# Taking the gate's column out of a matrix product: row sums on VectorE, POOL and ScalarE instead, and another order of work in the first output chunks

## The chip, the cores and the metric

The kernel runs on one core of a Trainium2 chip. The metric is the device time of one execution in microseconds (us). The engines of a core run their own instruction queues side by side: TensorE (PE in the profile, with PEld for its weight loads), VectorE (DVE), ScalarE (ACT), GpSimd (POOL) and SyncE (SP, which issues most of the transfers here). They wait for one another through semaphores.

## The reference

```python
def _A_ref(x, wqkv, wo):              # B, S, D = 1, 2048, 448; 16 heads of 28
    q, k, v = split_heads(x @ wqkv)
    pq, pk = phi(q), phi(k)           # phi(t) = where(t > 0, t + 1, exp(t)) + 1e-6
    kv = einsum("bhsd,bhse->bhde", pk, v)
    z = sum over s of pk
    o = (pq @ kv) / (pq . z + 1e-6)
    return merge_heads(o) @ wo

def _B_ref(u, ...):                   # S4D: a long causal convolution per column, plus u * D_skip
    ...

x = A_x
g = sigmoid((x * gate_w).sum(-1, keepdims=True))
return g * _A_ref(x, ...) + (1 - g) * _B_ref(x, ...)
```

There are 2048 rows of x with 448 columns. The gate g is one number for each row: a weighted sum of the row, put through a sigmoid. The change concerns how that weighted sum is computed.

## The kernel before

**Tiling.** The 2048 rows are handled as 16 chunks of 128 rows. Each chunk of x is loaded twice over in one transfer: turned (columns on the partitions, for use as a matmul operand) and plain (rows on the partitions). A float32 operand is split in a high part (a cast to the reduced format float32r, on ScalarE) and a low part (the rest, by a subtraction, mostly on POOL), and a product is made of three kinds of matmuls: high by high, low by high, high by low. One product of a chunk by a 448 x 448 matrix is 11 matmuls of 448 columns.

**The first stage** is a loop over c = 2 to 13, with the chunks before and after written out by hand. In iteration c the queues get, in this order:
- SP: the load of x for chunk c + 3 (`load_x`).
- PE: the k product of chunk c + 1 (11 matmuls), the q product of chunk c (11 matmuls), then `do_g` of chunk c (11 matmuls, which accumulate k's features times x in four PSUM banks).
- ACT and POOL: high and low parts of chunk c + 2 (`split_t` for the turned copy, `split_n` for the plain one), POOL's product of x with D_skip (`skip`).
- ACT and DVE: k's features of chunk c + 1 (`k_feature`, `k_high`, `k_low`) and q's of chunk c (`q_post`).
- DVE, in iterations 2 to 5: the preparation of the S4D part (`steps`), which ends with four small transposes on PE (line 319); in iterations 6 to 11 a running sum over chunks (`running`).

The order within each engine's queue is the order of the source (`manual_schedule`); a queue does not go on past an instruction that waits.

**Buffers.** x lies in a pool of four buffers (`xp`). Chunks 0, 1 and 2 share two of them: the first holds the turned chunk 2 and the plain chunk 0, the second the plain chunks 1 and 2. Chunks 3 and 4 have the other two, and the load of chunk 5 in iteration 2 needs one of these four again. A buffer is given out again when the last instruction that reads it, on whichever engine, is done. The k product goes to one of two PSUM banks (`v1` or `k`: in iterations 3, 5, 6 and 7 it is `k`), and the q product to one bank (`q`); the next product in the bank waits until the features are finished with it.

**The gate** is column 448 of the q product: the weights of q have 450 columns, with `gate_w` as column 448 and zeros in 449. `q_post` starts with ACT's exponential of that column into `e1[:, c]` (line 387); `gate(0, 15)` turns 15 columns of `e1` into 1 + exp(-s) and the factor `og` after the first stage, and the last chunk's follow in `late`, in the middle of the output stage.

**Between the stages**, `norm_a` to `norm_d` make the denominators and the normalised q of each chunk (POOL products, DVE reductions and reciprocals), and kv is multiplied by `wo` (`kv_products`, `m_products`). The 11 matmuls of the last q product are cut in pieces (`q_run`) and put where PE would otherwise wait.

**The output stage** goes over pairs of chunks (c, c + 1). Each pair is turned on PE (`turn_pe`), split in high and low parts (ACT and DVE: `turn_even`, `odd_high`, `odd_ends`, `odd_low`), multiplied in `attend` (11 matmuls of 448 columns for each chunk, line 676), and combined with the S4D part and sent out by `final_b` (DVE, SP).

Of the kernel before, what the change touches and what calls it, by code (L numbers as in the profile page):

```python
# [15 lines left out]
P = 128  # L16
S = 2048
D = 448
# [12 lines left out]
FIRST = 2 * NAT + J * D  # L31
QA = 1
QW = 512
# [108 lines left out]
@with_exitstack  # L142
def gated_mix_kernel(ctx: ExitStack, tc: tile.TileContext, xin, wq_d, wvo_d, abc_d, ldt_d, dsk_d,
                     turn_d, cst_d, first_d, gin_d, out):
# [24 lines left out]
    ones = const.tile([P, P], F32R, name="ones")  # L169
    dsk = const.tile([P, D], F32, name="dsk")  # L170
    side = []
# [33 lines left out]
    raw = yf[:, F0:]  # L205
    wqr = yf[:, F0 - J * (D + 2):F0].rearrange("p (j d) -> p j d", j=J)
    abc = [t[:DJ, o:o + 2 * J * N].rearrange("p (i j n) -> p i j n", i=2, j=J) for t, o in ((pf, 3 * J * N), (rf, 0))]
# [44 lines left out]
    def skip(c):  # L252
        POOL.tensor_tensor(out=y[:, c], in0=plain[c][:, :D], in1=dsk, op=ALU.mult)  # L253

    idle = ps.tile([P, 512], F32, name="q", tag="q")
# [88 lines left out]
    def project(*args, **kw):  # L344
        o, run = pieces(*args, **kw)
        run(11)
        return o
# [38 lines left out]
    def q_post(c, o, mid=None):  # L386
        ACT.activation(e1[:, c:c + 1], o[:, D:D + 1], AF.Exp, scale=-1.0)
        if c < 5 or c >= NC - 2:
            return feature(pq[:, c], o, mid, side[0][:, :D] if 1 < c < 5 else None)
        e = tp.tile([P, D], F32, name="e", tag="e")  # L390
        ACT.activation(e, o[:, :D], AF.Relu, scale=-1.0)
        ACT.activation(e, e, AF.Exp, scale=-1.0)
        ACT.add(e, e, 1e-6)
        DVE.scalar_tensor_tensor(out=pq[:, c], in0=o[:, :D], scalar=C1, in1=e, op0=ALU.add, op1=ALU.max)

    def do_q(c, tag="q"):
        q_post(c, project(c, wqh, wql, D + 2, tag))

    def gate(a, b):
        DVE.tensor_scalar(out=e1[:, a:b], in0=e1[:, a:b], scalar1=1.0, scalar2=None, op0=ALU.add)  # L400
        DVE.reciprocal(out=og[:, a:b], in_=e1[:, a:b])
        DVE.tensor_scalar(out=og[:, a:b], in0=og[:, a:b], scalar1=-1.0, scalar2=1.0, op0=ALU.mult, op1=ALU.add)

# [94 lines left out]
    k_low(2)  # L498
    qo = project(0, wqh, wql, D + 2, "q", "w")
    split_t(3)  # L500
    q_post(0, qo)
    split_n(2)
    qo = project(1, wqh, wql, D + 2, "v0")
    q_post(1, qo)
# [13 lines left out]
    for c in range(2, NC - 2):  # L518
# [12 lines left out]
        ko = project(c + 1, wkh, wkl, D, "v1" if c in (2, 4) or c > 6 and c % 2 == 0 else "k")  # L531
        rows = list(ROWS.get(c, ()))
        if c > 6 and rows:
            running(rows.pop(0))
        if c == 13:
# [17 lines left out]
        k_low(c + 1)  # L553
        if rows:
            running(rows.pop(0))
        qo = project(c, wqh, wql, D + 2, "q")
        q_post(c, qo)
        for i in rows:
            running(i)
        if c < 5:  # L560
            steps(2 if c == 4 else 1)
# [73 lines left out]

    def turn_even(c, o):
        t = xt_p.tile([P, 2, J, P], F32R, name="th", tag="t")
        th[c], tl[c] = t[:, 0], t[:, 1]
        ov = o.rearrange("p (j t) -> p j t", j=J)
        ACT.copy(th[c], ov)  # L640
        DVE.tensor_tensor(out=tl[c], in0=ov, in1=th[c].bitcast(F32), op=ALU.subtract)  # L641

    def turn_odd(c, o, oe):
        odd_high(c, o)
        odd_ends(c, 0, oe)
        odd_ends(c, 1, oe)
        odd_low(c, o)

# [16 lines left out]
    def attend(c, cuts):  # L665
        av[c] = []
        even = c // 2 * 2
        h, l, ends = th[c], tl[c], (th, tl)[c % 2][even + 1][:, 3]
        for i, (lo, hi) in enumerate(cuts):
            pool, tag = ((p3, "a"), (p3, "a"), (ps, "v0"), (ps, "k"))[(c + i) % 4]  # L670
            a = pool.tile([P, 512], F32, name="a", tag=tag)
            av[c].append((a, lo, hi))
            seq = [(u_[:, j], w_[:, j]) for j in (2, 0, 1) for u_, w_ in ((h, mh), (l, mh), (h, ml))]
            seq += [(ends, mh[:, 3]), (tl[even][:, 3], low_w3[c % 2])]
            for n, (u_, w_) in enumerate(seq):
                PE.matmul(a[:, lo:hi], lhsT=u_, rhs=w_[:, lo:hi], start=n == 0, stop=n == 10)  # L676
# [22 lines left out]
    zl = tp.tile([P, D], F32R, name="zl", tag="v0", bufs=1)  # L699
    qo = project(c, wqh, wql, D + 2, "q")  # L700
    do_g(c, (0, 1, 2))
# [9 lines left out]
    norm_a(1)  # L711
    gate(0, c + 1)
    norm_bd(0)
    norm_c(0)
    norm_a(2)
    for i in range(4):
        do_g(c + 1, (i,))
        ACT.copy(gs[i], g[i][:, :D])
        if i == 1:
            qo, q_run = pieces(c + 1, wqh, wql, D + 2, "q")  # L720
            q_run(2)
# [54 lines left out]

    q_run(1)
    k1 = kv_products(1)
# [21 lines left out]
    norm_a(4)  # L800
    turn_even(0, t0)
    odd_high(1, t1)
# [19 lines left out]
    def late():  # L822
        c = NC - 1
        yield
        e = tp.tile([P, D], F32, name="e", tag="e")
        t = tp.tile([P, D], F32, name="t", tag="t")
        ACT.activation(e1[:, c:], qo[:, D:D + 1], AF.Exp, scale=-1.0)
        ACT.activation(e, qo[:, :D], AF.Exp)
        yield
        DVE.tensor_scalar(out=e1[:, c:], in0=e1[:, c:], scalar1=1.0, scalar2=None, op0=ALU.add)  # L830
        DVE.tensor_scalar(out=t, in0=e, scalar1=1.0, scalar2=1e-6, op0=ALU.min, op1=ALU.add)
        DVE.reciprocal(out=og[:, c:], in_=e1[:, c:])
        yield
        DVE.tensor_scalar(out=og[:, c:], in0=og[:, c:], scalar1=-1.0, scalar2=1.0, op0=ALU.mult, op1=ALU.add)
        DVE.scalar_tensor_tensor(out=pq[:, c], in0=qo[:, :D], scalar=C1, in1=t, op0=ALU.add, op1=ALU.max)
# [7 lines left out]
    norm_b(5)  # L843
    norm_d(4, 2, ACT.copy)
    for c in range(2, NC, 2):
        more = c + 2 < NC
        final_b(c - 2)
        t0 = turn_pe(c)
        t1 = turn_pe(c + 1)
        if more:  # L850
            norm_c(c + 2)
        if c + 6 < NC:
            norm_a(c + 6)
        if c + 4 < NC:
            norm_b(c + 4)
        turn_even(c, t0)
        if more:
            norm_c(c + 3)
        if c + 6 < NC:
            norm_a(c + 7)  # L860
        turn_odd(c + 1, t1, t0)
# [28 lines left out]
def _layout(inputs):  # L890
# [16 lines left out]
    def tiles(w):  # L907
# [7 lines left out]
    w = np.asarray(inputs["A_wqkv"])  # L915
    wq = np.zeros((D, D + 2), np.float32)
    wq[:, :D] = w[:, :D]
    wq[:, D] = np.asarray(inputs["gate_w"])
    byd = lambda a: np.asarray(a).reshape(J, DJ, -1).transpose(1, 0, 2)
# [21 lines left out]
        f(byd(inputs["B_log_dt"])[:, :, 0]),  # L941
        f(np.asarray(inputs["B_D_skip"]).reshape(1, D)),
        f(np.stack([np.eye(P), lag >= 1], axis=1)),
# [20 lines left out]
```

## Time and profile before

| | |
|---|---|
| median of 3 runs | 168.7 us (168.25 to 168.81) |
| the profiled execution: its own time | 168.38 us |
| its span in the trace | 166.4 us |
| PE busy | 161.1 us, 97% of the span |
| DVE, ACT, POOL busy | 116.1, 109.4, 104.9 us |
| mean granted clock of PE | 0.997 of full |

All times within the execution count from the start of the span. The execution's own time is 2.0 us longer than the span, for what lies around it. A line of a timeline gives the start in us, the duration in us, the engine, the source line, the operation, output <- inputs with their shapes, the count of merged instructions, and in brackets the idle time of the engine ahead of it with the instruction that ended it. A line of the chain gives start, length, engine, tensor and source line. Matmuls overlap in the pipeline: one takes about 0.36 us, and the next starts 0.20 us after it.

### The profile page before, as it was taken

How to read it: one execution, taken by the hardware profiler on the slowest of the kernel's cores; microseconds unless marked ns; L12 is line 12 of the kernel's file. 1: busy time of each engine (PE TensorE's matmuls, PEld its weight loads, DVE VectorE, ACT ScalarE, POOL GpSimd, SP SyncE). 2: the span in 40 equal slices, each digit the busy share in tenths (PEclk: the TensorE clock that was granted, in tenths of full speed). 3: DMA queues.
4: the chain of work that ended last, by engine and by line, in shares of the span. 5: the costliest groups of instructions: out<-in, count | busy, mean ns of one | idle time of the engine just before them, and what ended most of it. 6: DMA issues, size and time to landing. Idle time of an engine off the chain costs nothing.

```text
span 166.4 us, 2609 instructions
## 1 busy us (share of the span) xinstructions
PE 161.1 (97%) x835; PEld 144.9 (87%) x835; DVE 116.1 (70%) x243; ACT 109.4 (66%) x257; POOL 104.9 (63%) x116
## 2 busy tenths in 40 slices
PE   6999999999999999999999999999999999999991
PEld 2698999999999999999999999988987999999990
DVE  0837753685852879889885555898899979986441
ACT  3688668988486784766758966453856766676541
POOL 3073589678809449477295999749689998633000
PEclk9999999999999999999999999999999999999998
DMA  5999966687974330959988007997121221122222
GB/s 157 411 314 321 287 143 230 228 295 276 336 255 136 126 107 19 221 141 250 295 261 165 0 4 117 185 203 161 27 46 55 110 110 55 61 110 110 110 78 95
DMA packets 10783, 27.51 MB, mean 165 GB/s; under 512 B 1328, under 2 KB 6992, under 8 KB 10544
## 3 DMA queue, kind: packets, MB, share of 16 engines
q1 hardware_dynamic: 8992, 21.71, 39.1%
q0 software_dynamic: 1632, 5.51, 17.6%
q8 instruction: 7, 0.11, 0.3%
q10 hardware_dynamic: 144, 0.11, 0.2%
q14 instruction: 8, 0.07, 0.1%
HBM read 17.87 MB, written 3.67 MB: 129 GB/s over the span
## 4 chain that ended last, share of the span: by engine, by line
PE 87%; DVE 6%; DMA 2%; ACT 1%; issue 1%; ACTq 0%; DVEq 0%
PE g L416 21%; PE q L340 19%; PE a L676 19%; PE v L340 12%; PE k L340 11%; PE tr L633 3%; DMA y<-in 2%; DVE den L601 2%; PE k L755 1%; DVE wk L743 1%; DVE th L641 1%; DVE ot L681 1%; ACT kvh L772 0%; DVE shl L743 0%; ACT wk L466 0%
## 5 line engine op out<-in xcount | busy, mean ns | idle before, releaser
L676 PE MATMUL a<-wk,th 128*128 128x448 f32 (+1 forms) x178 | 37.4, 357 | 0.3 <-DVE th L641 0.3
L416 PE MATMUL g<-pkh,xn 128*128 128x448 f32 x112 | 35.7, 364 | 0.0
L676 PEld LDWEIGHTS a<-wk,th 128*128 128x128 f32 x178 | 31.3, 188 | 2.9 <-DVE th L641 0.7
L237 POOL TENSOR_TENSOR xt<-xr,xt 128x512 fp32r<-128x512 f32 x14 | 18.2, 1298 | 19.8 <-ACT xt L241 19.8
L340 PE MATMUL q<-wqh,xt 128*128 128x450 f32 x120 | 27.8, 367 | 0.0
L237 POOL TENSOR_TENSOR xn<-xr,xn 128x448 fp32r<-128x448 f32 x16 | 19.6, 1228 | 10.1 <-ACT xn L247 10.1
L340 PEld LDWEIGHTS q<-wqh,xt 128*128 128x128 f32 x120 | 22.5, 189 | 1.8
L416 PE MATMUL g<-pkl,xn 128*128 128x448 f32 x64 | 23.3, 364 | 0.0
L416 PEld LDWEIGHTS g<-pkh,xn 128*128 128x128 f32 x112 | 21.1, 188 | 2.3
L596 POOL TENSOR_TENSOR prod<-pq,zb 128x448 f32<-128x448 f32 x16 | 18.3, 1154 | 4.5 <-ACT zb L709 2.9
L253 POOL TENSOR_TENSOR y<-xr,dsk 128x448 f32<-128x448 f32 x16 | 20.4, 1281 | 0.0
L340 PE MATMUL k<-wk,xt 128*128 128x448 f32 x88 | 19.7, 366 | 0.1
L340 PE MATMUL v<-wk,xt 128*128 128x448 f32 x88 | 18.9, 362 | 0.0
L340 PEld LDWEIGHTS k<-wk,xt 128*128 128x128 f32 x88 | 16.4, 188 | 2.0 <-ACT wk L466 0.5
L340 PEld LDWEIGHTS v<-wk,xt 128*128 128x128 f32 x88 | 16.5, 188 | 1.1
L681 DVE SCALAR_TENSOR_TENSOR ot<-y,og,a 128x448 f32<-128x448 f32 (+1 forms) x17 | 10.7, 626 | 7.5 <-PE a L676 7.3
L621 POOL TENSOR_TENSOR room<-pq,den 128x336 f32<-128x336 f32 x16 | 12.1, 756 | 5.4 <-issue 2.6
L687 ACT COPY pq<-a 128x448 f32<-128x448 f32 (+1 forms) x17 | 8.6, 512 | 5.8 <-DVE ot L681 5.6
L416 PEld LDWEIGHTS g<-pkl,xn 128*128 128x128 f32 x64 | 11.2, 174 | 1.1 <-DVE pkl L379 0.2
L656 ACT CAST th<-tr 64x128 fp32r<-64x128 f32 x32 | 8.3, 261 | 5.5 <-DVE th L641 5.1
L340 PE MATMUL q<-wql,xt 128*128 128x450 f32 x45 | 11.7, 366 | 0.0
L369 DVE SCALAR_TENSOR_TENSOR k<-k,e 128x448 f32<-128x448 f32 x8 | 5.1, 632 | 9.0 <-ACT e L368 8.8
(155 smaller groups left out, 289.7 us busy)
## 6 DMA issues: line engine op xcount, KB each, us to landing
xr<-in SPq DMA_DIRECT2D x15, 512.0 KB, 3.9
out<-ot SPq DMA_DIRECT2D x15, 224.0 KB, 1.9
room<-in SPq DMA_DIRECT2D x3, 896.0 KB, 7.5
wvo<-in SPq DMA_DIRECT2D x2, 896.0 KB, 5.5
y<-wvo POOLq DMA_DIRECT2D x2, 896.0 KB, 8.2
y<-room POOLq DMA_DIRECT2D x2, 896.0 KB, 9.2
y<-over POOLq DMA_DIRECT2D x2, 896.0 KB, 9.5
y<-in SPq DMA_DIRECT2D x2, 480.0 KB, 4.7
```

Of the source, the lines that this page charges most:

```text
L237: eng.tensor_tensor(out=o, in0=r, in1=h.bitcast(F32), op=ALU.subtract)
L253: POOL.tensor_tensor(out=y[:, c], in0=plain[c][:, :D], in1=dsk, op=ALU.mult)
L340: PE.matmul(o[:, :n], lhsT=a, rhs=b, start=run.n == 1, stop=not seq)
L369: DVE.scalar_tensor_tensor(out=pks[c], in0=pks[c], scalar=1.0, in1=e, op0=ALU.add, op1=ALU.max)
L416: PE.matmul(g[i][:a.shape[1], :D], lhsT=a, rhs=b, start=c == 0 and n == 0, stop=c == NC - 1 and n == len(seq) - 1)
L596: POOL.tensor_tensor(out=pd[c], in0=pq[:, c], in1=zb, op=ALU.mult)
L621: POOL.tensor_tensor(out=n[:, :3, :DJ].rearrange("p j (h d) -> p j h d", h=4), in0=a, in1=r[:, :H - 4].rearrange("p (j h) -> p j h", j=3)[ ...
L633: PE.transpose(o[:, j * P:(j + 1) * P], pn[c][:, j], ident)
L656: ACT.copy((th, tl)[i][c][half, 3], oe[i * DT:(i + 1) * DT, 3 * P:])
L676: PE.matmul(a[:, lo:hi], lhsT=u_, rhs=w_[:, lo:hi], start=n == 0, stop=n == 10)
L681: DVE.scalar_tensor_tensor(out=ot[:, lo:hi], in0=y[:, c, lo:hi], scalar=og[:, c:c + 1], in1=a[:, lo:hi], op0=ALU.mult, op1=ALU.add)
L687: ACT.copy(pq[:, c, lo:hi], a[:, lo:hi])
```

## The change

The gate's column leaves the q product, whose matmuls then have 448 columns instead of 450, and `gate_w` is loaded as a second row beside D_skip and spread over the partitions (`rows`, `gwt`). The weighted sum of a row is computed from the plain x in one of two ways:
- `gate_sum(c)` on DVE: one instruction that multiplies and sums along the row. Chunks 0 and 1 in iteration 2, chunks 2 and 3 in iteration 3, chunks 4 and 5 in iteration 4, chunk 14 in iteration 12, chunk 15 in iteration 13, each behind `q_post` of that iteration.
- `gate_products(c + 2)` on POOL at the end of iterations 4 to 11, and `gate_total(c + 1)` on ACT at the head of iterations 5 to 12, ahead of `split_t`: chunks 6 to 13.

One exponential of all 16 columns and one `gate()` follow the first stage; the parts for the last chunk in `late` go. In the second place the order of work changes: in the first output pairs the high parts are made earlier and the low part of chunk 2 stands ahead of `final_b`; `norm_d(2, 2)` and `norm_d(4, 2)` move; the 11 matmuls of `attend(0)` get another order; one more of the last q product's matmuls goes ahead of `kv_products`. The padding of one buffer changes, so that the sizes together stay as they were.

```diff
-PADS = 32
+PADS = 96
+SUMS = {2: (0, 1), 3: (2, 3), 4: (4, 5), 12: (14,), 13: (15,)}
...
-    wqh, wql = (const.tile([P, J, QW], F32R, name=n)[:, :, :D + 2] for n in ("wqh", "wql"))
+    wqh, wql = (const.tile([P, J, D], F32R, name=n) for n in ("wqh", "wql"))
...
-    SP.dma_start(out=dsk, in_=dsk_d.to_broadcast([P, D]))
+    SP.dma_start(out=rows, in_=rows_d.to_broadcast([P, 2, D]))
     load_x(3)
...
+    def gate_sum(c):
+        DVE.scalar_tensor_tensor(out=tp.tile([P, D], F32, name="t", tag="t"), in0=plain[c][:, :D], scalar=1.0, in1=gwt,
+                                 op0=ALU.mult, op1=ALU.mult, accum_out=e1[:, c:c + 1])
+
+    def gate_products(c):
+        POOL.tensor_tensor(out=prod[:, c % 3], in0=plain[c][:, :D], in1=gwt, op=ALU.mult)
+
+    def gate_total(c):
+        ACT.activation(prod[:, c % 3], prod[:, c % 3], AF.Copy, accum_out=e1[:, c:c + 1])
...
     def q_post(c, o, mid=None):
-        ACT.activation(e1[:, c:c + 1], o[:, D:D + 1], AF.Exp, scale=-1.0)
...
         ko = project(c + 1, wkh, wkl, D, "v1" if c in (2, 4) or c > 6 and c % 2 == 0 else "k")
...
+        if 4 < c < 13:
+            gate_total(c + 1)
...
-        qo = project(c, wqh, wql, D + 2, "q")
+        qo = project(c, wqh, wql, D, "q")
         q_post(c, qo)
...
+        for i in SUMS.get(c, ()):
+            gate_sum(i)
         if c < 5:
             steps(2 if c == 4 else 1)
...
+        if 3 < c < 12:
+            gate_products(c + 2)
...
-    gate(0, c + 1)
+    ACT.activation(e1, e1, AF.Exp, scale=-1.0)
+    gate()
...
-    q_run(1)
+    q_run(2)
     k1 = kv_products(1)
...
-    turn_even(0, t0)
+    even_high(0, t0)
     odd_high(1, t1)
...
+    norm_d(2, 2, ACT.copy)
     ACT.copy(mh[:DT, 3], shl[:DT, 0].bitcast(F32))
+    even_low(0, t0)
     odd_ends(1, 0, t0)
-    norm_d(2, 2, ACT.copy)
...
+            if c == 0:
+                seq = [seq[n] for n in (0, 2, 3, 6, 1, 4, 5, 7, 8)]
...
-    norm_d(4, 2, ACT.copy)
     for c in range(2, NC, 2):
         more = c + 2 < NC
-        final_b(c - 2)
         t0 = turn_pe(c)
         t1 = turn_pe(c + 1)
+        if c == 2:
+            even_high(c, t0)
+            odd_high(c + 1, t1)
+            norm_d(c + 2, 2, ACT.copy)
+            even_low(c, t0)
+        final_b(c - 2)
...
-        for _ in range({4: 1, 6: 2}.get(c, 0)):
+        for _ in range({4: 1, 6: 1}.get(c, 0)):
             next(later, None)
```

More of the change, by code (lines that the diff above doesn't have):

```diff
@@ L169, in gated_mix_kernel @@
     ones = const.tile([P, P], F32R, name="ones")
-    dsk = const.tile([P, D], F32, name="dsk")
+    rows = const.tile([P, 2, D], F32, name="rows")
+    dsk, gwt = rows[:, 0], rows[:, 1]
     side = []
@@ L396, in do_q, with gate @@
     def do_q(c, tag="q"):
[L397 to L402, printed above, removed]
+        q_post(c, project(c, wqh, wql, D, tag))
+    def gate():
+        DVE.tensor_scalar(out=e1, in0=e1, scalar1=1.0, scalar2=None, op0=ALU.add)
+        DVE.reciprocal(out=og, in_=e1)
+        DVE.tensor_scalar(out=og, in0=og, scalar1=-1.0, scalar2=1.0, op0=ALU.mult, op1=ALU.add)
     gps = ExitStack()
@@ L498, in gated_mix_kernel @@
     k_low(2)
-    qo = project(0, wqh, wql, D + 2, "q", "w")
+    qo = project(0, wqh, wql, D, "q", "w")
     split_t(3)
@@ L502, in gated_mix_kernel @@
     split_n(2)
-    qo = project(1, wqh, wql, D + 2, "v0")
+    qo = project(1, wqh, wql, D, "v0")
     q_post(1, qo)
@@ L531, in gated_mix_kernel @@
         ko = project(c + 1, wkh, wkl, D, "v1" if c in (2, 4) or c > 6 and c % 2 == 0 else "k")
-        rows = list(ROWS.get(c, ()))
-        if c > 6 and rows:
-            running(rows.pop(0))
+        todo = list(ROWS.get(c, ()))
+        if c > 6 and todo:
+            running(todo.pop(0))
+        if 4 < c < 13:
+            gate_total(c + 1)
         if c == 13:
@@ L553, in gated_mix_kernel @@
         k_low(c + 1)
-        if rows:
-            running(rows.pop(0))
-        qo = project(c, wqh, wql, D + 2, "q")
+        if todo:
+            running(todo.pop(0))
+        qo = project(c, wqh, wql, D, "q")
         q_post(c, qo)
-        for i in rows:
+        for i in todo:
             running(i)
+        for i in SUMS.get(c, ()):
+            gate_sum(i)
         if c < 5:
@@ L636, in turn_even, with even_high, even_low @@
     def turn_even(c, o):
+        even_high(c, o)
+        even_low(c, o)
+    def even_high(c, o):
         t = xt_p.tile([P, 2, J, P], F32R, name="th", tag="t")
         th[c], tl[c] = t[:, 0], t[:, 1]
[L639 to L647, printed above, removed]
+        ACT.copy(th[c], o.rearrange("p (j t) -> p j t", j=J))
+    def even_low(c, o):
+        DVE.tensor_tensor(out=tl[c], in0=o.rearrange("p (j t) -> p j t", j=J), in1=th[c].bitcast(F32), op=ALU.subtract)
     def odd_high(c, o):
@@ L719, in gated_mix_kernel @@
         if i == 1:
-            qo, q_run = pieces(c + 1, wqh, wql, D + 2, "q")
+            qo, q_run = pieces(c + 1, wqh, wql, D, "q")
             q_run(2)
@@ L855, in gated_mix_kernel @@
             norm_b(c + 4)
-        turn_even(c, t0)
-        if more:
-            norm_c(c + 3)
+        if c > 2:
+            turn_even(c, t0)
+            odd_high(c + 1, t1)
+            if more:
+                norm_c(c + 3)
         if c + 6 < NC:
             norm_a(c + 7)
-        turn_odd(c + 1, t1, t0)
+        for i in range(2):
+            odd_ends(c + 1, i, t0)
+        odd_low(c + 1, t1)
         final_c(c - 2)
```

21 lines of the change are left out of this document (7 added, 14 removed).

## The prediction, made before the changed kernel was run

> **What bounds the kernel now.** I read the page's busy times first, then the chain that ended last, then TensorE's waits, then the queues' timelines of the stretches where the change puts work.
>
> ```profile
> PE 161.1 (97%) x835; PEld 144.9 (87%) x835; DVE 116.1 (70%) x243; ACT 109.4 (66%) x257; POOL 104.9 (63%) x116
> 35.41 2.20 PE v L340 x11
> 37.61 2.21 PE q L340 x11
> 42.02 2.20 PE k L340 x11
> 44.22 2.27 PE q L340 x11
> 49.11 2.20 PE k L340 x11
> 55.72 2.20 PE k L340 x11
> 126.97 2.27 PE a L676 x10
> PEclk9999999999999999999999999999999999999998
> PE a L676 <- DVE th L641: 0.3, 1, 0.3
> ```
>
> TensorE (PE) is the path from 5 to 163 us: project after project follows without a gap, and behind the warm-up its waits hold 0.3 us, at the start of output chunk 2. So a removed matmul column counts in full and, more important here, each new wait of PE counts in full; the other engines' 30% of idle time is free only where nothing that PE needs stands behind the new work. That is what has to be looked for, queue by queue.
>
> In the chain, 35.41 is the k product of chunk 5 (k5), 37.61 q4, 42.02 k6, 44.22 q5, 49.11 k7, 55.72 k8; the chain counts a product from the end of the matmul before, so its first matmul starts up to 0.16 us earlier. These are the due times below.
>
> **x's buffers, where the change costs most.** x has four buffers. Which reader frees them?
>
> ```profile
> SPq L202 <- POOL y L253: 19.7, 5, 11.5
> 23.35 0.35 SPq L202 DMA_DIRECT2D xr<-in  x1
> 26.53 0.33 SPq L202 DMA_DIRECT2D xr<-in  x1
> 22.16 2.43 POOL L253 TENSOR_TENSOR y<-xr,dsk 128x448 f32<-128x448 f32 x2
> 25.35 1.16 POOL L237 TENSOR_TENSOR xn<-xr,xn 128x448 fp32r<-128x448 f32 x1 [0.76 <-ACT xn L247]
> DMA to landing us min/median/max: 3.1/3.4/12.5
> ```
>
> The load of chunk 5 (23.35) stood 11.5 us in SP's queue until POOL's skip product of chunk 0 was done (first half of the 22.16 pair); that of chunk 6 (26.53) came with the end of chunk 3's low part (25.35 + 1.16). A load starts when the last reader of a buffer is done, and lands 3.4 us later (median of line 202). The change gives chunks 0 to 5 a later reader, the gate sum on VectorE (DVE): chunks 0 and 1 in iteration 2, chunks 2 and 3 in iteration 3, chunks 4 and 5 in iteration 4, each behind that iteration's q features. All four buffers (x0 with the turned x2; x1 with x2; x3; x4) then wait for one of them.
>
> ```profile
> 30.46 0.68 DVE L296 SCALAR_TENSOR_TENSOR y<-room,pq 112x512 f32<-112x512 f32 x1
> 31.18 0.69 DVE L296 SCALAR_TENSOR_TENSOR y<-room,pq 112x512 f32<-112x512 f32 x1
> 31.48 0.61 ACT L241 CAST xt<-xr 128x512 fp32r<-128x512 f32 x1
> 32.85 1.29 POOL L237 TENSOR_TENSOR xt<-xr,xt 128x512 fp32r<-128x512 f32 x1
> 36.21 0.63 DVE L360 SCALAR_TENSOR_TENSOR pq<-q,t 128x448 f32<-128x448 f32 x1
> 43.04 0.16 DVE L281 TENSOR_TENSOR sums<-sm,sums 112x4 f32<-112x4 f32 x1
> 45.70 0.14 DVE L315 TENSOR_REDUCE oks<-okc 112x1 f32<-112x4 f32 x1
> 47.53 0.61 DVE L379 SCALAR_TENSOR_TENSOR zb<-k,zb 128x448 f32<-128x448 f32 x1
> 47.54 0.55 PE L319 MATMUL p<-both,sm 112*128 112x112 f32 x4
> ```
>
> A gate sum has the form of line 296 (two inputs, sum along the row): 0.72 us from one to the next at 512 columns, so 0.70 at 448.
> - Chunk 5: line 360 of q2 leaves DVE free at 30.46, so sum 0 is done at 31.15; the load starts at 31.2 instead of 23.35 and lands at 34.6. ScalarE (ACT) stood at this chunk's cast at 31.48 and now waits 3.1 us; behind it in its queue are chunk 4's k features, q3's exponential, and the sums of the S4D preparation. Cast 0.61, then POOL's low part 1.3: 36.5. k5's second matmul, due at 35.6, needs it: PE waits 0.9.
> - q4 needs the q bank, freed when DVE ends line 360 for q3. From the cast to that end the queues took 31.48 to 36.84, 5.3 us without the exponential of the gate column, and it was all dependent work. 34.6 + 5.3 = 39.9, due at 37.6 + 0.9: 1.4 more, 2.3 in all.
> - Chunk 6: next free is the buffer of x1 and x2, after sum 2, which stands behind that same line 360: 39.8 + 0.7 = 40.5. It lands at 44.0, its low part is ready at 45.9; k6's second matmul is due at 42.2 + 2.3 = 44.5: 1.4, in all 3.7.
> - q5 by the same chain of instructions: 44.0 + 5.3 = 49.3 against 44.2 + 3.7 = 47.9: 1.4, in all 5.1.
> - Then DVE has sums 4 and 5 (1.4), and behind them the 15 small instructions of S4D (43.04 to 45.84, 2.8), which the transposes of line 319 need: 49.2 + 1.4 + 2.8 = 53.4, due at 47.5 + 5.1 = 52.6: 0.8, in all 5.9.
> - k7 reuses k6's bank, freed by line 379, whose chain starts behind the small instructions: 45.70 to 48.14 is 2.4; 53.3 + 2.4 = 55.7, due at 48.95 + 5.9 = 54.85: 0.9, in all 6.8.
>
> Later loads are not late: chunk 7 takes x3's buffer at 41.2 and is used at about 51; chunks 8 and 9 follow at about 50 and are used from 60 on. SP's half loads of x queue behind them; they are first used in iteration 6.
>
> **The products on POOL and their totals on ACT** (chunks 6 to 13). A total stands on ACT ahead of the next cast. Prices: the product as POOL's low part of the same size (49.70 below), 1.16 us; the total as ACT's summing pair of line 294, 0.63 + 0.19 at 512 columns and overlapping a little, so 0.7 at 448.
>
> ```profile
> 46.41 0.55 ACT L373 ACTIVATE pkh<-k 128x448 fp32r<-128x448 f32 x1 [1.00 <-DVE k L369]
> 49.00 0.62 ACT L247 CAST xn<-xr 128x512 fp32r<-128x512 f32 x1
> 49.70 1.16 POOL L237 TENSOR_TENSOR xn<-xr,xn 128x448 fp32r<-128x448 f32 x1 [4.19 <-ACT xn L247]
> 29.79 0.63 ACT L294 ACTIVATE y<-pq 112x512 f32<-112x512 f32 x1
> 30.33 0.19 ACT L294 ACTIVATION_READ_ACCUMULATOR y<-pq 112x1 f32 x1
> 51.35 0.55 ACT L367 ACTIVATE e<-k 128x448 f32<-128x448 f32 x1 [0.69 <-PE k L340]
> 54.32 0.61 DVE L379 SCALAR_TENSOR_TENSOR pkl<-k,pkh 128x448 fp32r<-128x448 f32 x1
> 71.25 0.55 ACT L367 ACTIVATE e<-k 128x448 f32<-128x448 f32 x1 [1.45 <-PE k L340]
> ```
>
> Chunk 7 is the tight one: ACT's natural cast (49.00), POOL's low part (49.70), now the product, and only then ACT's total. In the shifted time: pkh of chunk 6 at 54.0, natural cast 2.55 later (as 46.41 to 49.00), 56.55; POOL 57.25 to 59.5; total to 60.2; two casts, 61.3; then from line 367 to the end of line 379 as before (51.35 to 54.93, 3.6): 64.9. k8 reuses k7's bank and is due at 55.6 + 6.8 = 62.4: 2.4, in all 9.2. Alone, without the shift, it is 2.2 by the same rows (POOL 52.0, total 52.7, casts 53.8, bank 57.4 with 55.55 due, and up to 0.4 for the running sum's first copy).
>
> From chunk 8 on I count nothing: ACT waits 1.45 us per chunk for PE's k product (71.25), which covers the total's 0.7, and POOL's four pieces (1.3 + 3 x 1.16) fit in the 6.6 us of a chunk. POOL's group additions (up to 1 us more, in three chunks) use the rest of that cover; without it a chunk would give back 0.3 to 0.5.
>
> **The small terms.**
>
> ```profile
> 18.49 1.30 POOL L237 TENSOR_TENSOR xt<-xr,xt 128x512 fp32r<-128x512 f32 x1 [0.39 <-ACT xt L241]
> 19.82 4.48 PE v L340 x22
> 108.75 0.36 PE L705 MATMUL zo<-zh,ones 128*128 128x448 f32 x1
> 107.96 0.57 ACT L703 CAST zh<-zb 128x448 fp32r<-128x448 f32 x1 [0.69 <-DVE zb L379]
> 124.88 0.61 DVE L681 SCALAR_TENSOR_TENSOR ot<-y,og,a 128x448 f32<-128x448 f32 x1
> 126.24 0.68 DVE L641 TENSOR_TENSOR th<-tr,th 128x512 fp32r<-128x512 f32 x1
> 126.26 0.37 PE L676 MATMUL a<-wk,th 128*128 128x448 f32 x1
> ```
>
> The broadcast load ahead of chunk 3's grows by a row of 224 KB. At line 202's 512 KB in 3.4 us that delays what follows by at most 1.5 us, and chunk 3's low part was ready at 19.8 for k3, the second half of the 22 matmuls from 19.82, so at 22.0: hidden by 2.2.
>
> Sum 15 stands on DVE ahead of chunk 15's features, which were started without slack; line 705 had 0.2 us of slack behind line 703, so PE waits 0.45 there. In the output stage the low part of chunk 2 (126.24) is moved ahead of the output product of line 681, so it starts near 124.9 and ends at 125.6; PE's second matmul of the chunk, the one that stood at 126.97, can follow the first (126.26) at 126.46: 0.5 gained. If ACT's cast were not earlier too, 0. The single gate for all chunks waits for ACT's exponential behind line 709 and starts 0.35 later; the added q matmul ahead of line 755 (0.2) and the moved work cover it. Columns: 176 q matmuls lose 2 of 450. 11 of either width take 2.20 us in the chain (42.02 against 37.61, 2.21): 0 to 0.15 by these rows; I take 0.1.
> The Trainium skill (TensorE: Matmul & The Clock Gate, "Wait — 56ns, not 53.3ns?") gives a warm matmul as its columns at 2.4 GHz plus a fixed 2.5 ns; by that the columns bring 0.15 us (an estimate: 176 x 2 / 2.4 GHz), inside the bounds of the rows, though the rows' 200 ns per matmul is above the page's 189.
>
> **Sum.** 9.2 + 0.45 - 0.5 - 0.1 = 9.0 on the profiled execution's 168.38 us: 177.4 us. That execution lies 0.3 below the median of the three (168.7); I say 177.5.
>
> **Rivals.**
> 1. Loads on time: another buffer frees in time for chunks 5 and 6, and only k8's wait is left: 168.4 + 2.2 = 170.6. Against it: no buffer is without a gate sum. It decides if chunk 5's load starts before 28.1 (31.48 - 3.4).
> 2. Faster: the added instructions do not hold their queues where they are written, but run in idle time. Then nothing waits, and the output stage's 0.5 and the columns' 0.1 remain: 167.8. It needs sum 0 to end before 28.1. Against it: DVE, ACT and SP ran in written order wherever I looked.
> 3. The clock drops. PE's granted clock was full in every slice but the last, without a wait over 0.5 behind the start. The new waits reach 2.4 us.
> The Trainium skill (the same page, "What's actually happening") has the clock fall to half after an idle window of about 3.4 us. By that a 2.4 us wait need not trigger it, and no run here shows one.
> If it halved for 3.4 us, PE would lose 1.7 us (half of a stretch as long as a q and a part of g): 179.2.
> 4. One of the two late loads costs little (PE finds its low part in time): about 2.3 to 2.8 less, 175.
>
> **Numbers.** The forecast (both loads late and the total late) 0.72, its own range 175.5 to 180: two landings at 3.1 us (line 202's least) take 0.6 off, a moved reduction or cast that overlaps less takes or adds 0.2 at some six places (1.2), and a landing behind a half load may add 1. Rival 1: 0.10; rival 2: 0.06; rival 3: 0.06; rival 4: 0.06. About 0.3% (0.5 us) is what can be told from no change here; of rival 1 and 2, 0.03 lie within it. The range 172.0 to 180.5 leaves out rivals 1 and 2 and the tail of 3. Faster 0.06, same 0.04, slower 0.90.
>
> **What would show it.** Chunk 5's load at 31 instead of 23.35 and chunk 6's near 40; ACT waiting some 3 us at line 241 for a DMA, twice; PE waits at k5, q4, k6, q5, line 319, k7, k8 of 0.5 to 2.5 us each between 35 and 65; ACT waiting 2.5 us for POOL ahead of a total near 58; none of it after 70; the wait for line 641 near 127 gone, one of 0.4 at line 705. Wrong it is if chunk 5's load starts near 23, if ACT's queue is not in written order, or if PE's idle time before 70 stays under 3 us.

## The result, and the profile after

| | before | after |
|---|---|---|
| median of six runs | 168.69 us (168.25 to 168.86) | 178.31 us (177.87 to 178.92) |
| ratio | | 1.057, 95% interval 1.0552 to 1.0589 |
| the profiled execution, its span | 168.38, 166.4 us | 178.21, 176.3 us |

The change costs 9.6 us (9.8 between the two profiled executions); 177.5 us was predicted, from a sum of 9.0. Lines move down in the changed kernel: 319 is now 329, 340 is 350, 360 is 370, 379 is 389, 641 is 661, 676 is 692, 705 is 721; the gate sum is line 256, POOL's product 260, ACT's total 263. From the page after, PE's busy time and its granted clock in 40 slices:

```profile
PE 162.7 (92%) x835; PEld 144.5 (82%) x835; DVE 122.9 (70%) x256; ACT 113.6 (64%) x258; POOL 115.9 (66%) x124
...
PEclk9999999999999999999999999999999999999999
```

As many matmuls as before (835), 1.6 us more busy time (161.1 before) and 8.3 us more idle time, in a span 9.9 us longer, at full clock: PE waits. Most of the added busy time lies at the waits: a matmul takes 0.36 us, of which the next one covers all but 0.20, and ahead of a wait nothing covers it. So a wait sets PE back by more than its length in the list (k8 falls behind k7 by 2.43 in the table below, and its wait is 2.18). Its waits after (us in all, times, longest; the wait for the warm-up data at the start is left out):

```profile
PE k L350 <- DVE pkl L389: 2.2, 1, 2.2
PE q L350 <- DVE pq L370: 2.1, 2, 1.0
...
PE p L329 <- DVE oks L325: 1.0, 1, 1.0
PE zo L721 <- ACT zh L719: 0.9, 1, 0.9
PE v L350 <- POOL xt L237: 0.9, 1, 0.9
PE k L350 <- POOL xt L237: 0.9, 1, 0.9
PE k L350 <- DVE zb L389: 0.8, 1, 0.8
...
```

Where they stand, from PE's timeline after (start, duration, and in brackets the idle time ahead and what ended it):

```profile
36.41 2.28 PE L350 MATMUL v<-wk,xt 128*128 128x448 f32 x10 [0.88 <-POOL xt L237]
...
39.74 1.88 PE L350 MATMUL q<-wqh,xt 128*128 128x448 f32 x8 [1.04 <-DVE pq L370]
...
45.77 2.28 PE L350 MATMUL k<-wk,xt 128*128 128x448 f32 x10 [0.88 <-POOL xt L237]
...
49.10 1.88 PE L350 MATMUL q<-wqh,xt 128*128 128x448 f32 x8 [1.04 <-DVE pq L370]
...
53.79 0.60 PE L329 MATMUL p<-both,sm 112*128 112x112 f32 x4 [1.01 <-DVE oks L325]
...
56.25 2.45 PE L350 MATMUL k<-wk,xt 128*128 128x448 f32 x11 [0.83 <-DVE zb L389]
...
65.28 2.44 PE L350 MATMUL k<-wk,xt 128*128 128x448 f32 x11 [2.18 <-DVE pkl L389]
...
119.28 0.47 PE L721 MATMUL zo<-zh,ones 128*128 128x448 f32 x1 [0.94 <-ACT zh L719]
```

These are the seven places named in the prediction, in its order, and line 705 (now 721) behind them. What releases them begins in two queues. SP's timeline after (loads of chunks 5 and 6), then ACT's (its waits for the landings and for POOL's products):

```profile
31.00 0.35 SPq L202 DMA_DIRECT2D xr<-in  x1
...
40.35 0.33 SPq L202 DMA_DIRECT2D xr<-in  x1
```

```profile
34.39 0.62 ACT L241 CAST xt<-xr 128x512 fp32r<-128x512 f32 x1 [3.04 <-DMA xr<-in]
...
43.75 0.62 ACT L241 CAST xt<-xr 128x512 fp32r<-128x512 f32 x1 [3.03 <-DMA xr<-in]
...
59.95 0.58 ACT L263 ACTIVATE prod<-prod 128x448 f32<-128x448 f32 x1 [2.45 <-POOL prod L260]
```

Chunk 5's load left at 31.00 (23.35 before), chunk 6's at 40.35, ACT stood about 3 us for each, and 2.45 us for POOL ahead of a total.

The place where PE stands against the trace before, step by step (the start of the same matmul in both traces):

| PE at | before | after | later by | predicted |
|---|---|---|---|---|
| q4 | 37.45 | 39.74 | 2.29 | 2.3 |
| k6, second matmul | 42.05 | 45.77 | 3.72 | 3.7 |
| q5 | 44.05 | 49.10 | 5.05 | 5.1 |
| transposes of line 319 | 47.54 | 53.79 | 6.25 | 5.9 |
| k7 | 48.95 | 56.25 | 7.30 | 6.8 |
| k8 | 55.55 | 65.28 | 9.73 | 9.2 |
| zo | 108.75 | 119.28 | 10.53 | 9.65 |
| last matmul | 162.57 | 172.72 | 10.15 | 9.15 (9.05 with the columns) |

Behind the last matmul the final transfers were 0.25 shorter: 9.9 for the span.

### The profile page after: what moved, and what is told of

Same layout as the page of the kernel before. It is cut to its first block, busy times and chain, and to the rows that moved or that the text cites. A ratio compares the mean times of both kernels' runs of the same rounds, so it can differ in the third digit from the quotient of the medians.

```text
span 176.3 us, 2620 instructions
## 1 busy us (share of the span) xinstructions
PE 162.7 (92%) x835; PEld 144.5 (82%) x835; DVE 122.9 (70%) x256; ACT 113.6 (64%) x258; POOL 115.9 (66%) x124
## 4 chain that ended last, share of the span: by engine, by line
PE 33%; DVE 17%; ACT 12%; issue 2%; DMA 1%; SPq 0%; ACTq 0%; DVEq 0%
PE a L692 20%; PE tr L648 3%; PE g L425 3%; PE k L350 3%; PE q L350 2%; ACT pkh L383 2%; DVE room L444 2%; DVE r L443 2%; DVE k L379 1%; ACT e L378 1%; PE v L350 1%; DMA wk<-shl 1%; ACT e L377 1%; DVE room L465 1%; DVE y L465 1%
## 5 line engine op out<-in xcount | busy, mean ns | idle before, releaser
L350 PE MATMUL q<-wqh,xt 128*128 128x448 f32 x120 | 27.6, 365 | 2.1 <-DVE pq L370 2.1
L237 POOL TENSOR_TENSOR xn<-xr,xn 128x448 fp32r<-128x448 f32 x16 | 20.3, 1270 | 10.4 <-ACT xn L247 8.8
L350 PE MATMUL k<-wk,xt 128*128 128x448 f32 x88 | 20.8, 378 | 3.9 <-DVE pkl L389 2.2
L253 POOL TENSOR_TENSOR y<-xr,rows 128x448 f32<-128x448 f32 x16 | 20.3, 1279 | 0.0
L241 ACT CAST xt<-xr 128x512 fp32r<-128x512 f32 x14 | 8.6, 611 | 6.4 <-DMA xr<-in 6.4
L350 PE MATMUL q<-wql,xt 128*128 128x448 f32 x45 | 11.6, 362 | 0.0
```

The source lines that it names most:

```text
L237: eng.tensor_tensor(out=o, in0=r, in1=h.bitcast(F32), op=ALU.subtract)
L241: ACT.copy(w[:, :NAT], turned[c])
L350: PE.matmul(o[:, :n], lhsT=a, rhs=b, start=run.n == 1, stop=not seq)
```

## The experiments

### Do the gate sums of x make the loads late?

In `e1_sums_free` the sums of chunks 0 to 5 read a constant row and no chunk of x, so they hold no buffer (those gates come out as other numbers); in `e1b_first_load` only chunks 2 to 5 do.

```diff
-  in0=plain[c][:, :D]
+  in0=dsk if c < 6 else plain[c][:, :D]          # e1_sums_free
+  in0=dsk if 1 < c < 6 else plain[c][:, :D]      # e1b_first_load
```

> The gate sums of chunks 0 to 5 stay where they are on VectorE, with the same shape and time, but read the D_skip row instead of x (so these six chunks get a wrong gate): x's four buffers get no later reader. Theory (the buffers, not the work): chunk 5's load starts near 23 again, the waits of TensorE at k5, q4, k6, q5, line 329 and k7 go, and what remains over the kernel before is k8's wait (2.2 us) and the one at the column sums of z (1.0): 171 us. Rival (the added work itself on VectorE, and its contention with POOL, costs the time): about 178, as after the change.

> As the run before, but the sums of chunks 0 and 1 read x again; only those of chunks 2 to 5 read the D_skip row. Theory: chunk 5's load still starts at 31 behind sum 0, and costs 0.9 at k5 and 1.4 at q4; chunk 6's load follows at once into chunk 3's buffer, lands by 35 and costs nothing: 171 + 2.3 = 173.3 us. If one late load were enough to put the whole stage out of step, near 178; if it were hidden, 171.

Measured: `e1_sums_free` 175.24 us (173.02, 174.56, 175.91, 179.19), `e1b_first_load` 174.24 us, ratio to before 1.0355 (1.0313 to 1.0396); before beside them 168.5. PE's waits in `e1_sums_free`:

```profile
PE k L350 <- DVE pkl L389: 2.2, 1, 2.2
...
PE p L329 <- DVE oks L325: 1.0, 1, 1.0
PE zo L721 <- ACT zh L719: 1.0, 1, 1.0
PE k L350 <- DVE zb L389: 0.8, 1, 0.8
...
```

The four waits at k5, q4, k6 and q5 are gone, so the sums' reading of x caused them. Chunk 5's load left when it did before:

```profile
23.30 0.35 SPq L202 DMA_DIRECT2D xr<-in  x1
```

Three things came out otherwise than expected. The waits at the transposes (p) and k7 stayed although no load was late. In `e1b_first_load` PE waited for no load either: chunk 5's left at 26.13, with the end of chunk 3's low part on POOL (24.94 + 1.16), so it took chunk 3's buffer. Chunk 6's left at 30.62, behind sum 0, and still came in time.

```profile
26.13 0.35 SPq L202 DMA_DIRECT2D xr<-in  x1
```

With late readers on two of the four buffers no load came too late; with late readers on all four, in the changed kernel, two did (three buffers were not tried). So the 174.24 us lie near the 173.3 expected by chance: the two waits expected, 2.3 us, did not come, and those at p and k7 and a slower clock stand in their place. That clock is the third thing. Windows of `e1_sums_free` (busy time of PE, PEld, DVE, ACT, POOL, then PE's granted clock, DMA share, GB/s):

```profile
58.00:60.00 2.00, 0.00 (x0) 0.00 (x0) 1.39 (x4) 1.79 (x4) 2.00 (x3) 1.00 0.00 0
60.00:62.00 2.00, 1.95 (x8) 1.78 (x9) 1.56 (x3) 1.97 (x6) 0.62 (x1) 0.76 0.27 41
62.00:64.00 2.00, 2.00 (x7) 1.78 (x6) 1.81 (x4) 0.74 (x2) 1.96 (x2) 0.50 0.56 221
64.00:66.00 2.00, 2.00 (x11) 1.85 (x10) 0.63 (x1) 1.27 (x3) 2.00 (x3) 0.89 0.00 0
```

PE waited 2.17 us ahead of k8 (until 60.05) and in the 6 us behind it ran about 3.4 us at 0.50 (from the clocks 0.76, 0.50 and 0.89 of three windows of 2 us: 0.96, 2.0 and 0.44 us at half). Its four runs had mean granted clocks of 1.0 (173.02 us), 0.990, 0.987 and 0.978 (179.19 us). The run at full clock is explained by the waits that are left: 168.5 + 2.2 + 1.0 + 1.0 + 0.8 - 0.5 (output stage) = 173.0.

### The totals on ACT

```diff
-        if 4 < c < 13:            # ahead of split_t, split_n
-            gate_total(c + 1)
         ...
         q_post(c, qo)
         ...
+        if 4 < c < 13:
+            gate_total(c + 1)
```

> ScalarE's gate totals stand behind q_post of their iteration instead of ahead of split_t; nothing else is changed. Theory: POOL's product is long done when the total's turn comes, so ScalarE doesn't wait 2.5 us ahead of chunk 8's cast, k7's bank is free in time, and TensorE's 2.2 us at k8 goes, while the late loads still cost their 7.3: 176.0 us. Rival (ScalarE's added 0.7 us per chunk is the cost, wherever it stands): no gain, 178.3.

Measured: 176.19 us, ratio 1.0439 (1.0404 to 1.0474). k8's wait is gone from the list of waits, and those of q (2.1 in all), p, zo (1.1), v and k stay as in the changed kernel: 2.1 us less, as expected.

Both edits together:

> Both edits together: sums of chunks 0 to 5 on the D_skip row (their gates wrong), and the totals behind q_post. Theory: no wait of TensorE between 28 and 65 us; left are 1.0 us at the column sums of z behind sum 15, the columns' gain and the output stage's new order: 168.4 + 1.0 - 0.4 = 169.0 us. If the two causes overlap (each alone hides the other), the gain is less than the sum of the two runs before.

Measured: 171.86 us, ratio 1.0228 (1.0156 to 1.03). The expectation of 169.0 missed by what the first experiment had already shown in part: waits of 1.0 at zo, 1.0 at p, 0.8 at k7, and a new one of 0.9 at line 752. None of them hangs on a load or a total.

### The sums as work on VectorE

`e5_later_sums` moves sums 4 and 5 out of iteration 4 and sum 15 out of iteration 13:

```diff
-SUMS = {2: (0, 1), 3: (2, 3), 4: (4, 5), 12: (14,), 13: (15,)}
+SUMS = {2: (0, 1), 3: (2, 3), 5: (4, 5), 12: (14, 15)}       # on top of e3_both
```

> The third experiment's last one (gate sums of chunks 0 to 5 on a constant row in place of x, ACT's totals behind q's features; 171.9) with the sums of iteration 4 moved to iteration 5 and that of chunk 15 to iteration 12. Theory: the waits of 1.0 at the transposes of line 329 and 0.8 at k7 come from the two sums of iteration 4 on VectorE, and the 1.0 at zo from chunk 15's sum ahead of the last features: all three go, 171.9 - 1.8 - 1.0 = 169.0. Rival: they are the price of the extra VectorE work wherever it stands, and come back in iterations 5 and 12: 171 to 172.

Measured: 171.75 us, ratio 1.0184 (1.0158 to 1.021). The waits at p, k7 and zo are gone, as the theory said, and did not come back in iteration 5. But one of 2.73 took their place, at q14, so that the time is the rival's (171 to 172): for sums 14 and 15 in iteration 12 the rival was right. From VectorE's and POOL's timelines of this run:

```profile
97.28 2.71 DVE L256 SCALAR_TENSOR_TENSOR t<-xr,rows 128x448 f32<-128x448 f32 x1
```

```profile
96.82 2.69 POOL L237 TENSOR_TENSOR wo<-wvo,wo 112x448 fp32r<-112x448 f32 x2
```

This is chunk 15's sum. Where a sum stands alone it takes 0.62; here it lasted 2.71, ending 0.5 behind POOL's pair of subtractions (the low parts of `wo`). The changed kernel has the same thing, smaller; its VectorE, then its POOL:

```profile
49.50 1.57 DVE L256 SCALAR_TENSOR_TENSOR t<-xr,rows 128x448 f32<-128x448 f32 x1
...
113.80 1.04 DVE L256 SCALAR_TENSOR_TENSOR t<-xr,rows 128x448 f32<-128x448 f32 x1
```

```profile
48.99 1.58 POOL L260 TENSOR_TENSOR prod<-xr,rows 128x448 f32<-128x448 f32 x1
...
112.18 2.17 POOL L253 TENSOR_TENSOR y<-xr,rows 128x448 f32<-128x448 f32 x1
```

The first is chunk 5's sum, ahead of the transposes; the second chunk 15's, ahead of zo. Both end about 0.5 behind the POOL instruction beside them. So far this is only a coincidence in time; `b1p_psum_operand` below tests it.

The reverse test adds only the sums of chunks 0 to 5 to the kernel before, into a column that nobody reads:

```diff
+        for i in {2: (0, 1), 3: (2, 3), 4: (4, 5)}.get(c, ()):
+            gate_sum(i)            # in0=plain[i], in1=dsk, sum to a spare column
```

> The kernel before with the gate sums of chunks 0 to 5 added on VectorE at the changed kernel's places, reading x, into a column that nobody reads; the gate column stays in q's products, no POOL product, no total on ACT, no sum of the last chunks. Theory: the loads of chunks 5 and 6 go late as in the changed kernel (q4 +2.3, q5 +5.0 in all) and the transposes and k7 add 1.8: about 175. Rival: the loads need the POOL and ACT parts too, and only VectorE's added work shows: 169 to 170.3.

Measured: 176.92 us, ratio 1.0498 (1.0466 to 1.053): +8.2, 1.9 above the theory's 175. Its waits are those of the changed kernel up to k7 (and one of 0.4 in the first project), and k7 starts 7.75 later than before (56.70 against 48.95; 7.30 in the changed kernel). So six VectorE instructions of 0.6 us make more than four fifths of the loss by themselves.

### The output stage alone

> The kernel before with the output stage's new order alone; the gate column and everything ahead of that stage stay. The prediction's step gave this part -0.5, so 168.0 by it. Theory now, from the trace after: the wait for line 641's low part (0.6) goes, the second chunk pair's transposes gain 0.2, but attend(0) in its new order reaches the product with the rows that a late transfer brings earlier and loses 0.7: -0.1, so 168.4.

> As the one before, with attend(0)'s first nine products in the order 0, 2, 3, 1, 4, 5, 6, 7, 8, so that those which need the late transfer's rows come last. If attend(0)'s loss in the changed kernel comes from its own order, it is given back: about -0.8 against the kernel before, 167.7. If the transfer is awaited whatever the order, 168.4 as in the run beside it.

`e4b` differs by one line:

```diff
-                seq = [seq[n] for n in (0, 2, 3, 6, 1, 4, 5, 7, 8)]
+                seq = [seq[n] for n in (0, 2, 3, 1, 4, 5, 6, 7, 8)]
```

Measured: `e4_output_only` 168.10 us, ratio 0.9966 (0.9951 to 0.9981), so 0.6 faster; `e4b_other_order` 167.44, ratio 0.9924 (0.9903 to 0.9945), 1.3 faster. PE's timeline at attend(0), first of `e4_output_only`, then of `e4b_other_order`:

```profile
120.51 1.02 PE L677 MATMUL a<-wk,th 128*128 128x448 f32 x3
121.73 1.85 PE L677 MATMUL a<-wk,th 128*128 128x448 f32 x8 [0.19 <-DMA wk<-shl]
```

```profile
120.41 2.67 PE L677 MATMUL a<-wk,th 128*128 128x448 f32 x11
```

The prediction's 0.5 stood. The expectation of 0.1, worked out afterwards, had left out that one q matmul moves into the wait ahead of the kv products (one matmul, 0.2); the remaining 0.3 is not explained. In the changed order attend(0) comes to the rows of the transfer wk<-shl early and takes 2.91 up to the next transposes (123.42); with those rows last it takes 2.51 (122.92).

### The work in the gaps, and what holds VectorE

`b1_sums_in_gaps` keeps all of the changed kernel's work and moves it:

```diff
-SUMS = {2: (0, 1), 3: (2, 3), 4: (4, 5), 12: (14,), 13: (15,)}
+SUMS = {2: (3, 2), 3: (4,), 5: (5,)}
+PRODUCTS = {c: (c + 2,) for c in range(4, 10)}
+PRODUCTS.update({10: (12, 13), 11: (14,)})
...
     q_post(1, qo)
+    gate_sum(0)
+    gate_sum(1)
...
             under(room[:, G + 2:])
+            gate_sum(15)           # iteration 13
...
+        for i in PRODUCTS.get(c - 1, ()):
+            gate_total(i)          # behind q_post(c)
...
```

The gate's exponential moves to the end of iteration 13, and attend(0) has the order of `e4b`. `b1p_psum_operand` differs from it in one operand (chunk 15's gate comes out as another number):

```diff
-            gate_sum(15)               # in0=plain[15], in1=gwt: both in SBUF
+            gate_sum(15, sums[0])      # in1: a row in PSUM
```

> The changed kernel with all of its work, the gate's parts moved to where both VectorE and POOL were idle before: sums 0 and 1 behind q1's features, 3 and 2 in iteration 2, 4 in iteration 3, 5 in iteration 5, 15 in iteration 13 behind the two room additions; POOL products for 6 to 14, of which 13 and 14 one iteration earlier, their totals on ACT behind q's features; the gate's exponential at the end of iteration 13; attend(0) in the other order of e4b. If the loss was the place of the sums and not the work, the loads leave at about 26.5, 33 and 37.5, no wait of PE over 0.4 is left up to the output stage, and it takes e4b's 167.4 less at most 0.3 for the columns: 167.1 to 167.6. If the added work costs wherever it stands: 169 or more.

> The kernel b1 with one operand of chunk 15's sum replaced: it reads the row in PSUM that the room additions beside it read, in place of the gate's row in SBUF (so that chunk's gate is another number). Engine, place, size and what waits for it are the same. In b1 this one instruction lasted 7.25 us (97.75 to 105.0), from inside POOL's stretch of back-to-back work to that stretch's end at 104.5, and TensorE then waited 4.0 us and ran at half clock for some 3 us. If VectorE is held because it reads two SBUF operands while POOL works on SBUF: about 0.6 to 0.7, no wait of TensorE, clock 1.0, and 173.3 - 4.0 - 1.6 to 2.3 of half clock = 167.0 to 167.7. If it is held by something else at that place (the chunk's data, the queue): 7 again and 173.3.

Measured: `b1_sums_in_gaps` 173.31 us, ratio 1.0265 (1.0235 to 1.0296). That is in the range of the rival (169 or more), but not by its cause, as one sum alone makes the loss; `b1p_psum_operand` 167.71, ratio 0.9964 (0.9941 to 0.9987), as expected if the operand's place matters. In `b1_sums_in_gaps` every wait of the changed kernel was gone, and beside 0.4 at line 460 one of 3.98 had come, behind chunk 15's sum. Its VectorE, then its POOL, then PE and its clock:

```profile
97.75 7.25 DVE L258 SCALAR_TENSOR_TENSOR t<-xr,rows 128x448 f32<-128x448 f32 x1
```

```profile
96.25 2.31 POOL L239 TENSOR_TENSOR wo<-wvo,wo 112x448 fp32r<-112x448 f32 x2
98.51 1.31 POOL L239 TENSOR_TENSOR xt<-xr,xt 128x512 fp32r<-128x512 f32 x1
99.74 2.50 POOL L464 DMA_DIRECT2D y<-over  x2
101.33 2.09 POOL L239 TENSOR_TENSOR xn<-xr,xn 128x448 fp32r<-128x448 f32 x1
102.45 2.07 POOL L255 TENSOR_TENSOR y<-xr,rows 128x448 f32<-128x448 f32 x1
104.81 0.90 POOL L449 DMA_DIRECT2D y<-room  x1 [0.30 <-POOL y L255]
```

```profile
108.50 3.36 PE L352 MATMUL q<-wqh,xt 128*128 128x448 f32 x8 [3.98 <-DVE pq L405]
```

```profile
PEclk9999999999999999999999999579999999999999
```

POOL works without a gap from 96.25 to 104.52 and stands from then to 104.81. The sum begins inside this stretch and ends at 105.0, 0.48 us behind the stretch's end. With one operand in PSUM, beside the same POOL work (VectorE, then POOL):

```profile
97.95 0.61 DVE L258 SCALAR_TENSOR_TENSOR t<-xr,v 128x448 f32<-128x448 f32 x1
```

```profile
96.43 2.34 POOL L239 TENSOR_TENSOR wo<-wvo,wo 112x448 fp32r<-112x448 f32 x2
98.69 1.33 POOL L239 TENSOR_TENSOR xt<-xr,xt 128x512 fp32r<-128x512 f32 x1
```

7.25 against 0.61, by where one operand lies: this shows the cause of the hold, and with it went PE's wait and the slow clock (5.6 us between the two medians, 5.1 by their ratios to the kernel before; 4.0 of it the wait).
The Trainium skill (SBUF — State Buffer, "Who interferes with whom") says that a VectorE instruction with two SBUF inputs contends with a GpSimd instruction that reads SBUF. The Trainium skill (the same page, "Summary: rules for kernel authors") adds that the second of the two to issue is blocked until the first has finished. The pair of runs agrees on who is held. It differs on how long: the sum was held through POOL's work of five rows above, not to the end of the one instruction that ran when it began.

The last version takes chunk 15's sum to iteration 11, into a gap of POOL, and chunks 11 to 14 wholly to POOL's products; `b2_column_kept` is `e4b_other_order` again, with the gate's column in q's products:

```diff
+PRODUCTS = {c: (c + 2,) for c in range(4, 9)}
+PRODUCTS.update({9: (11, 12), 10: (13, 14)})
...
+        for i in {10: (13, 14), 11: (15,), 12: ()}.get(c, (c + 3,)):
+            if i < NC:
+                load_x(i)          # loads 14 and 15 an iteration earlier
...
+        if c == 11:
+            gate_sum(15)           # behind k_low(12)
```

> All of the changed kernel's work, and b1's order but for chunks 11 to 15: POOL products of 11 and 12 at the end of iteration 9, of 13 and 14 at the end of iteration 10, their totals an iteration later, the loads of chunks 14 and 15 one iteration earlier in the program, and chunk 15's sum on VectorE in iteration 11, inside POOL's gap there (87 to 89.4 in b1). If a two-operand VectorE instruction is free where POOL is idle, no wait of TensorE over 0.4 is left: 167.0 to 167.7, level with the gate column kept (167.4 to 168.0). If the added work itself costs: 169 or more.

> The same kernel as e4b (gate column kept in q's products, the output stage's other order), beside b1 on one chip: 167.4. What b1 stands below it is all that taking the gate column out can be worth here: 0 to 0.3 expected, since the q products took 1.76 for eight matmuls with 448 columns and 1.77 with 450.

Measured: `b3_gaps_of_pool` 167.14 us, ratio 0.992 (0.9898 to 0.9942); `b2_column_kept` 167.97, ratio 0.9948 (0.9926 to 0.9971), after 167.44 and 0.9924 (0.9903 to 0.9945) for the same code as `e4b_other_order`. Chunk 15's sum in `b3_gaps_of_pool` (it began 0.3 us ahead of the end of POOL's skip product, at 88.75), and the only wait of PE there behind the first projects, which had one of 0.7:

```profile
88.44 0.79 DVE L258 SCALAR_TENSOR_TENSOR t<-xr,rows 128x448 f32<-128x448 f32 x1
```

```profile
PE v L460 <- POOL sums L239: 0.4, 1, 0.4
```

All of the changed kernel's work is done and 11 us of its time are gone. Against the column kept in q's products the times can't be told apart: the three intervals overlap. The traces can tell more. The prediction shows q4 (2.21) and q5 (2.27) of the kernel before, 11 matmuls of 450 columns each; with 448 columns, from the chain of the changed kernel:

```profile
67.73 2.20 PE q L350 x11
```

In `b2_column_kept` eight of 15 q products took 2.24 to 2.28 and the others 2.20 or 2.21, in all 0.55 above 15 times 2.20; in `b3_gaps_of_pool` each took 2.20 or 2.21. So q's narrower products do bring PE about half a microsecond, of which the wait of 0.4 at line 460, which `b2_column_kept` has not, takes most back. The rest of what makes these kernels faster than the one before is the output stage's new order, which `e4b_other_order` and `b2_column_kept` have by itself.

## Why the prediction was right, point by point

- **x's buffers.** Right in place, cause and size: loads at 31.00 and 40.35 (31.2 and 40.5 said), 2.29, 3.72 and 5.05 behind at q4, k6 and q5 (2.3, 3.7 and 5.1). `e1_sums_free` removes exactly the four waits at k5, q4, k6 and q5. With both loads late and PE waiting for each, rivals 1, 2 and 4 fell. The bound by which rival 1 would decide (a load before 28.1) agrees: with the load at 26.13 in `e1b_first_load` none of the four waits came. Two figures of the prediction slip by 0.1 from one of its lines to the next (39.9 to 39.8, 53.4 to 53.3); no term hangs on that.
- **The transposes and k7.** Right within 0.5, with a term mis-sized and its cause mixed up. The step "DVE has sums 4 and 5 (1.4)" took 0.54 + 1.50 = 2.04 to the next instruction, the second beside POOL's product. The sums began at 48.96 and not at 49.2, which gives 0.24 back, so the transposes came 0.35 later than said. The other 0.15 at k7 is the time from the end of line 389 (56.10) to PE's first matmul (56.25), which the prediction left out. And both waits were told as the end of the loads' chain. They are not: with loads on time they come all the same (1.0 and 0.8 in `e1_sums_free` and `e3_both`) and go when the sums leave iteration 4 (`e5_later_sums`). So the price of rival 1, loads on time, was too low: 173.0, and not 170.6.
- **k8.** By the table 2.43 more behind than k7, 2.4 said (the prediction's own figures, 64.9 against 62.4, give 2.5); `e2_totals_later` takes away this wait and no other of the list.
- **Nothing from chunk 8 on.** Right up to zo: k15 stood 9.51 behind where k8 stood 9.73. The 0.22 given back agree with q's narrower products (q7, q9 and q11 took 2.26 or 2.27 before and 2.20 after).
- **zo.** Mis-sized: 0.45 said; a wait of 0.94, 0.80 behind k8 in all. Sum 15 was counted at 0.70 to the next instruction and took 0.97 beside POOL's skip product.
- **The output stage.** 0.5 said, 0.38 in the trace (10.53 to 10.15), 0.6 measured alone. The wait for line 641 is gone as said; what the new order of attend(0) costs was not seen, nor what the moved q matmul brings.
- **The columns.** Mis-sized: 0.1 said, about 0.57 in the trace. The bounds of 0 to 0.15 rest on q4's 2.21 alone, while the same lines of the prediction have q5 at 2.27. In the kernel before eight of 15 whole q products took 2.26 to 2.28, the others 2.20 or 2.21: 0.57 above 15 times 2.20. After, each took 2.20 or 2.19 but for two behind a wait. The gain shows early: q0 began 0.10 later than before (17.49 against 17.39), k5 0.15 earlier (35.10 against 35.25). Why eight of the products and not all were longer stays open, and so does whether the two columns did it: the rows of `wqh` and `wql` in SBUF went from 512 numbers to 448 with them.
- **Rival 3, the clock.** It did not come in the changed kernel: clock 1.0 in all six runs, with a wait of 2.18. It did in three of four runs of `e1_sums_free` and in all four of `e1b_first_load` (mean clock 0.99); in their traces the wait is 2.17 and 2.18. Which of the two happens is not settled by these runs. One run of `e3_both` had a mean clock of 0.986 too; the traced run of that kernel, at 0.999, has no wait over 1.0 behind the start, and what PE waited in the other is not known.
The Trainium skill (TensorE: Matmul & The Clock Gate, "What's actually happening") has an activity window of some 3.4 us that runs freely and does not start with the kernel. The time at half clock here, 3.4 us, agrees; that the clock halved behind 2.17 us of idle time does not agree with a whole window of idleness, and that the same wait did so in one kernel and not in another would fit a free window's phase, which no run here shows.

The sum of 9.0 against 9.8 between the profiled executions (178.21 - 168.38): 0.5 more came up to k8, 0.35 more at zo, and the final transfers gave 0.25 back. Most of the first two is one error, a duration taken from a row where VectorE stood beside an idle POOL (line 296 at 30.46). That the total came so close is in part luck: without the 0.57 that q's narrower products gave back, the rest of the sum would have come to 10.4 (9.8 + 0.57, an estimate from the traces), where the prediction had 9.15. So the waits and the columns' gain were both set too low, and the two errors partly cancel.

## What to carry to other kernels

Before an instruction is added in an engine's idle time, list every resource that its operands hold: here six sums of 0.6 us cost 8 us, most of it because they became the last readers of all four load buffers. A VectorE instruction's duration is only as good as the row it is taken from: with two operands in SBUF, look at what POOL does in that stretch, and put it in a gap of POOL's or take one operand from PSUM. What the placed work can bring at best should be measured ahead of the placing: here the column's removal brought PE about half a microsecond, less than the times of these runs can tell apart, and the new order of the output stage 0.7 to 1.3 us.

## What the runs showed of the hardware

- A VectorE instruction with two SBUF operands (128 x 448, 0.62 us alone) lasted 1.04, 1.57, 2.71 and 7.25 us when it began beside POOL work, each time to about 0.5 us behind a POOL instruction's end; with one operand in PSUM, 0.61 in the same place. POOL's product grew from 1.15 to 1.58 beside it.
- A small instruction was held too, and in this pair of runs 10 ns in the order of the starts made the difference. VectorE's addition to the gate's 16 columns and POOL's pair of products of the denominators, in `e3_both` (VectorE, POOL), then in `e5_later_sums` (VectorE, POOL):

```profile
113.76 1.18 DVE L409 TENSOR_SCALAR e<-e 128x16 f32<-128x16 f32 x1 [0.28 <-ACT e L728]
```

```profile
113.75 2.27 POOL L611 TENSOR_TENSOR prod<-pq,zb 128x448 f32<-128x448 f32 x2 [3.60 <-ACT e L728]
```

```profile
114.02 0.18 DVE L409 TENSOR_SCALAR e<-e 128x16 f32<-128x16 f32 x1 [0.28 <-ACT e L728]
```

```profile
114.02 2.32 POOL L611 TENSOR_TENSOR prod<-pq,zb 128x448 f32<-128x448 f32 x2 [3.06 <-ACT e L728]
```

  Started behind POOL's product it took 1.18 us, started with it 0.18. The 1.0 goes on through VectorE's queue to `kvh` and is the new wait of 0.9 at line 752 in `e3_both`.
- A q product of 11 matmuls took 2.20 us with 448 columns; with 450 some took 2.20 and others up to 2.28 (the rows of the weights in SBUF were longer too, 512 numbers against 448).
- PE's clock can halve around an idle time of 2.17 us and stay so for 3.4 us. In `b1_sums_in_gaps`, with an idle time of 3.98 us, it did in each of six runs (mean clocks 0.980 to 0.988).
